# Starting every SBUF tile on a multiple of 128 bytes instead of 32 bytes past one

## The chip, the cores and the metric

The kernel runs on one core of one Trainium2 chip. The metric is the device time of one execution in microseconds (us), as the median of several runs. One core has five engines that matter here: TensorE (PE in the profile, its weight loads PEld), VectorE (DVE), ScalarE (ACT), GpSimd (POOL) and SyncE (SP), which issues every DMA of this kernel. SBUF is the on-chip memory that all of them work from. It has 128 partitions, and a tile occupies the same byte range in each of them, so one number, the tile's start address in bytes, says where it lies.

## The reference

```python
k_p = k.reshape(B, H, Sp, 8, D).mean(axis=3)      # q, k, v: (8, 8, 576, 64)
v_p = v.reshape(B, H, Sp, 8, D).mean(axis=3)
scores = scale * np.matmul(q, k_p.transpose(0, 1, 3, 2))
attn = softmax(scores)                             # over Sp = 72 pooled keys
x = np.matmul(attn, v_p)                           # -> (4608 tokens, 512)
...
h = x @ w_in                                       # 512 -> 2048
g = np.where(h >= 1, h, np.where(h <= -1, 0.0, (h + 1) ** 2 / 4))
x = g @ w_out                                      # 2048 -> 512
...
h = x @ w_in2
r = np.maximum(h, 0.0)
out = (r * r) @ w_out2
```

An attention over pooled keys and values is followed by two feed-forward layers, each 512 to 2048 to 512, over 4608 tokens, all in fp32.

## The kernel before

**Stages.** In the first 40 us the kernel loads k, v, q and the first weights and does the attention of the first 512 tokens. Then come 9 blocks of 512 tokens of the first layer, 16 steps each (`steps`). A step is one `gemm1` (line 675, 128 hidden columns) and, two steps later, one `gemm2` (line 747). Attention of the tokens ahead (lines 319 to 510) is put into slots between the steps, and the second layer's weights are prepared and written to DRAM. Block 0 of the second layer runs through the same two functions with weights streamed back into tiles `wt`. The other 8 blocks of the second layer are done in pairs by a seven-product (Strassen) scheme, whose matmuls stand at line 1017 (first product) and line 1026 (second product).

**Matmuls.** Accuracy is kept by splitting each operand into a rounded high part and a remainder, both of type fp32r, and multiplying three times: high by high, low by high, high by low. Every such matmul has a 128x128 stationary operand (512 bytes per partition) and 512 moving columns (2048 bytes per partition):

```python
for a, c in ((wh, xh), (wh, xl), (wl, xh)):
    ...
    nc.tensor.matmul(out=ph, lhsT=a[:, kk % a.shape[1], :], rhs=c[:, kk, :], ...)
```

The moving operand is one run of 2048 bytes, except in `gemm2` of the second layer's block 0. There the weights move, and they are two runs of 1024 bytes, 2048 bytes apart, of a `wt` tile. The first 10 steps of `gemm2` (line 736) use plain fp32 operands and one matmul instead of three.

**Where tiles lie.** Each matmul pairs tiles from pools that grow from the left (low) end of SBUF or from the right (high) end. Left: `cv` (staged weights `st`, `cb`, `z`), `xp` (`xhi`, `xlo`), `gp` (`gh`, `gl`), `ap`, `ac`, `kvp`, `at`, `wq` (`wt`) and, in the Strassen part, `gq`, `gs` (`gh`, `gl` again) and `tp`. Right: `wp`, `ws` (`wihi`, `wilo`, `wohi`, `wolo`) and, in the Strassen part, `wr` (`w`), `xc` (`x`) and `xt`. The left end begins with the pool `const`, which holds `ident` (512 bytes) and then `warm`, a constant of 4 bytes that takes a slot of 32:

```python
edge = ctx.enter_context(tc.tile_pool(name="edge", bufs=1, side="right"))
edge.tile([P, 16], F32, name="edge")
...
warm = const.tile([P, 1], F32, name="warm")
```

`const` begins at byte 16,512, which is 129 x 128, so the first pool after it begins at 16,512 + 512 + 32 = 17,056, which is 32 past a multiple of 128. At the right end the tile `edge`, which nothing reads or writes, keeps 64 bytes free, so that `wp` begins at byte 163,744, also 32 past a multiple of 128. Nearly every other tile has a size that is a multiple of 128 bytes and so inherits the 32. Only `ident` starts on a multiple of 128, and 54 tiles of 32 bytes in the pool `at` take all four residues in turn.

**Order.** Instruction order on each engine is fixed by the program. Address overlaps between pools that are closed and pools that take their place decide which instruction waits for which.

Of the kernel before, what the change touches and what calls it, by code (L numbers as in the profile page):

```python
# [10 lines left out]
F32 = mybir.dt.float32  # L11
# [22 lines left out]
def pooled_attention_moe_moe(  # L34
# [17 lines left out]
    P = 128  # L52
# [11 lines left out]
    const = ctx.enter_context(tc.tile_pool(name="const", bufs=1))  # L64
# [1 line left out]
    left, right, attn = ExitStack(), ExitStack(), ExitStack()  # L66

    edge = ctx.enter_context(tc.tile_pool(name="edge", bufs=1, side="right"))
    edge.tile([P, 16], F32, name="edge")
    wp = right.enter_context(tc.tile_pool(name="wp", bufs=1, side="right"))  # L70
    ws = right.enter_context(tc.tile_pool(name="ws", bufs=2, side="right"))
    cv = left.enter_context(tc.tile_pool(name="cv", bufs=4))
# [21 lines left out]

    ON_PE = 2
    NK = -(-SP // TR)
    warm = const.tile([P, 1], F32, name="warm")
    pad = [ac.tile([P, NK, H, TR], F32, name=f"pad{i}") for i in range(2)]

    def runs(t0, n):  # L100
# [1073 lines left out]
```

## Time and profile before

| | |
|---|---|
| median of 3 runs | 1637.45 us (1637.22 to 1638.47) |
| profiled execution | 1638.23 us, its span 1636.4 us |
| mean granted TensorE clock | 0.996 |
| busy share of the span | PE 99%, PEld 80%, DVE 77%, ACT 55%, POOL 7% |
| DMA | 284.67 MB, mean 174 GB/s |

The span runs from the first to the last instruction; 1.8 us of the execution's time lie around it. PE's busy time contains the modelled ends of pipelined matmuls, so its rate is read from starts: the time of a group of matmuls in the chain of work divided by their number.

### The profile page before, as it was taken

Reading aid. Unit: us, or ns where it says so; the run is one execution under the profiler, and the core shown is the slowest. Engines: PE = TensorE matmul, PEld = TensorE weight load, DVE = VectorE, ACT = ScalarE, POOL = GpSimd, SP = SyncE. Lnnn points to the kernel's source line nnn. Section 1 sums busy time; section 2 is a strip of 40 time slices with the busy share of each in tenths; the row PEclk is TensorE's granted clock in tenths of the full one; section 3 lists DMA queues with packets and bytes.
Section 4 is the critical chain, followed back from the end, with each engine's and each line's share of the span. In section 5 each row is a group of like instructions: output and inputs, shape, how many; then the busy total and the mean of one; then the engine's idle time right before and its main releaser. Section 6 shows DMA issues by size and latency. Waiting matters only on the chain.

```text
span 1636.4 us, 23224 instructions
## 1 busy us (share of the span) xinstructions
PE 1614.0 (99%) x7824; PEld 1314.2 (80%) x7824; DVE 1259.9 (77%) x2230; ACT 896.7 (55%) x1612; POOL 107.4 (7%) x91
## 2 busy tenths in 40 slices
PE   7999999999999999999999999999999999999998
PEld 6667888888878888888888888888888888888886
DVE  6999888898898988898885452579558855975585
ACT  6665556666666666666675532345435533553353
POOL 1442001011001000000100000000000000000000
PEclk9999999999999999999999999999999999999999
DMA  9565335545454554544370284667676776758564
GB/s 244 175 202 133 97 75 167 155 153 155 138 159 144 164 148 134 155 147 160 130 270 7 88 280 148 194 217 210 194 255 220 209 233 213 224 180 252 195 206 132
DMA packets 246725, 284.67 MB, mean 174 GB/s; under 512 B 121168, under 2 KB 149840, under 8 KB 246608
## 3 DMA queue, kind: packets, MB, share of 16 engines
q1 hardware_dynamic: 246608, 283.21, 56.5%
q8 instruction: 62, 1.02, 0.3%
q14 instruction: 55, 0.45, 0.1%
HBM read 218.10 MB, written 65.01 MB: 173 GB/s over the span
## 4 chain that ended last, share of the span: by engine, by line
PE 92%; DVE 4%; ACT 1%; DMA 1%; issue 1%; SPq 0%; POOL 0%; DVEq 0%; ACTq 0%; POOLq 0%
PE ph L675 25%; PE acc L747 25%; PE cp L1017 10%; PE dp L1026 10%; PE dq L1026 5%; PE cr L1017 5%; PE cq L1017 3%; PE dr L1026 3%; PE px L497 2%; PE pss L381 2%; PE acc L736 1%; DVE wi L155 0%; DMA kv<-in_k_dram 0%; DVE wilo L233 0%; DMA st<-in_moe_w_in_dram 0%
## 5 line engine op out<-in xcount | busy, mean ns | idle before, releaser
L675 PE MATMUL ph<-xhi,wihi 128*128 128x512 f32 x576 | 229.9, 399 | 0.9 <-ACT xhi L509 0.9
L974 ACT ACTIVATE gh<-g 128x512 fp32r<-128x512 f32 x224 | 140.7, 632 | 155.0 <-DVE g L1043 48.0
L675 PE MATMUL ph<-xlo,wihi 128*128 128x512 f32 x576 | 224.6, 390 | 0.0
L675 PE MATMUL ph<-xhi,wilo 128*128 128x512 f32 x576 | 224.5, 390 | 0.0
L747 PE MATMUL acc<-gh,wohi 128*128 128x512 f32 x536 | 215.8, 403 | 0.0
L747 PE MATMUL acc<-gl,wohi 128*128 128x512 f32 x536 | 209.5, 391 | 0.0
L747 PE MATMUL acc<-gh,wolo 128*128 128x512 f32 x536 | 209.0, 390 | 0.0
L782 DVE TENSOR_TENSOR gl<-g,gh 128x512 fp32r<-128x512 f32 x224 | 151.9, 688 | 49.6 <-ACT gh L974 48.1
L1017 PE MATMUL cp<-x,w 128*128 128x512 f32 x768 | 186.2, 390 | 0.2
L1017 PEld LDWEIGHTS cp<-x,w 128*128 128x128 f32 x768 | 143.9, 188 | 31.3 <-ACT s L1039 1.4
L1026 PE MATMUL dp<-gh,w 128*128 128x512 f32 x512 | 161.6, 389 | 0.0
L229 ACT ACTIVATE wihi<-wi 128x512 fp32r<-128x512 f32 x144 | 90.6, 629 | 122.0 <-PE ph L675 118.9
L233 DVE TENSOR_TENSOR wilo<-wi,wihi 128x512 fp32r<-128x512 f32 x144 | 104.4, 725 | 47.3 <-ACT wihi L229 46.9
L675 PEld LDWEIGHTS ph<-xhi,wihi 128*128 128x128 f32 x576 | 108.0, 188 | 27.8 <-issue 3.7
L675 PEld LDWEIGHTS ph<-xhi,wilo 128*128 128x128 f32 x576 | 108.1, 188 | 23.2 <-issue 0.2
L675 PEld LDWEIGHTS ph<-xlo,wihi 128*128 128x128 f32 x576 | 108.2, 188 | 21.8 <-issue 0.5
L1039 ACT ACTIVATE s<-cp 128x512 f32<-128x512 f32 x96 | 57.2, 596 | 116.4 <-PE cp L1017 116.4
L710 ACT ACTIVATE gh<-g 128x512 fp32r<-128x512 f32 x134 | 84.4, 630 | 66.3 <-DVE g L708 64.5
L747 PEld LDWEIGHTS acc<-gl,wohi 128*128 128x128 f32 x536 | 100.6, 188 | 22.4
L716 DVE TENSOR_TENSOR gl<-g,gh 128x512 fp32r<-128x512 f32 x150 | 103.4, 690 | 18.5 <-ACT gh L710 15.9
L747 PEld LDWEIGHTS acc<-gh,wohi 128*128 128x128 f32 x536 | 100.7, 188 | 20.4 <-issue 1.0
L747 PEld LDWEIGHTS acc<-gh,wolo 128*128 128x128 f32 x536 | 100.8, 188 | 19.4
(144 smaller groups left out, 3015.5 us busy)
## 6 DMA issues: line engine op xcount, KB each, us to landing
w<-w2i SPq DMA_DIRECT2D x224, 256.0 KB
w<-w2o SPq DMA_DIRECT2D x224, 256.0 KB
w2i<-cb SPq DMA_DIRECT2D x32, 512.0 KB
w2o<-cb SPq DMA_DIRECT2D x32, 512.0 KB
st<-in_moe_w_out_dram SPq DMA_DIRECT2D x31, 512.0 KB
st<-in_moe_w_in_dram SPq DMA_DIRECT2D x29, 512.0 KB
pd<-pad SPq DMA_DIRECT2D x32, 384.0 KB
z<-pd SPq DMA_DIRECT2D x96, 128.0 KB
```

The costliest lines, as they stand in the source:

```text
L229: nc.scalar.activation(out=hi, in_=src, func=AF.Copy)
L233: eng.tensor_tensor(out=lo, in0=src, in1=hi.bitcast(F32), op=ALU.subtract)
L381: nc.tensor.matmul(out=pss[off:off + n, i, :], lhsT=qT[t][:, p, off:off + n], rhs=kbd[b % 2][:, p, :], start=True, stop=True,)
L675: nc.tensor.matmul(out=ph, lhsT=a[:, kk % a.shape[1], :], rhs=c[:, kk, :], start=(i == 0), stop=(i == 3 * KD - 1))
L710: act(out=gh, in_=g, func=AF.Copy)
L716: nc.vector.tensor_tensor(out=gl, in0=g, in1=gh.bitcast(F32), op=ALU.subtract)
L747: nc.tensor.matmul(out=o, lhsT=lhsT, rhs=rhs, start=(f == 0 and x == 0), stop=(f == KF - 1 and x == 2),)
L782: tt(out=out, in0=a, in1=b, op=ALU.subtract)
L974: act(out=hi, in_=a, func=AF.Copy)
L1017: nc.tensor.matmul(out=out[0], lhsT=w[:, a, k, :], rhs=xq[b, i][c][:, k, :], start=(n == 0 and i in (1, 2, 7)), stop=(n == 5), skip_group_ ...
L1026: nc.tensor.matmul(out=out[d], lhsT=w[:, a, d, :], rhs=x[c], start=(g == 0 and n == 0 and i in (1, 2, 7, 4)), stop=(g == NG - 1 and n == 2 ...
L1039: act(out=snaps[key], in_=a, func=AF.Copy)
```

## The change

```diff
     edge = ctx.enter_context(tc.tile_pool(name="edge", bufs=1, side="right"))
-    edge.tile([P, 16], F32, name="edge")
+    edge.tile([P, 24], F32, name="edge")
...
-    warm = const.tile([P, 1], F32, name="warm")
+    warm = const.tile([P, 32], F32, name="warm")[:, 0:1]
```

`warm` takes 128 bytes where it took a slot of 32, so every tile on the left side moves up by 96 bytes: `cv` begins at 17,152 = 134 x 128. `edge` keeps 96 bytes free where it kept 64, so every tile on the right side moves down by 32 bytes: `wp` begins at 163,712 = 1279 x 128. In the built program all tiles except 54 of the 32-byte tiles in `at` then begin on a multiple of 128. The instructions of every engine, their order and the semaphores that they wait for are the same, row for row, in both programs, so no piece of the order is shown: only addresses differ. Between two tiles on the same side nothing changes; between a left tile and a right tile the distance shrinks by 128 bytes.

## Rows read from the trace of the kernel before

**Rows 1.** The profile's page: span, busy times, chain that ended last by engine.
```profile
span 1636.4 us, 23224 instructions
...
PE 1614.0 (99%) x7824; PEld 1314.2 (80%) x7824; DVE 1259.9 (77%) x2230; ACT 896.7 (55%) x1612; POOL 107.4 (7%) x91
...
PE 92%; DVE 4%; ACT 1%; DMA 1%; issue 1%; SPq 0%; POOL 0%; DVEq 0%; ACTq 0%; POOLq 0%
```

**Rows 2.** Busy time of each engine by stage (columns in the first line).
```profile
core 0: us, PE busy (x) PEld busy (x) DVE busy (x) ACT busy (x) POOL busy (x), PEclk, DMA share, GB/s
0.00:40.00 40.00, 31.15 (x245) 27.38 (x245) 23.79 (x56) 23.96 (x71) 6.57 (x14) 0.91 0.99 243
40.00:120.00 80.00, 75.19 (x462) 50.63 (x464) 78.81 (x127) 51.40 (x96) 38.95 (x24) 1.00 0.64 189
...
200.00:830.00 630.00, 630.00 (x3207) 514.30 (x3205) 561.84 (x1088) 411.51 (x750) 50.31 (x45) 1.00 0.48 148
...
1020.00:1636.40 616.40, 608.95 (x2683) 502.90 (x2681) 427.32 (x673) 275.34 (x458) 0.00 (x0) 1.00 0.67 209
```

**Rows 3.** Chain that ended last, in order of time: start us, us, work.
```profile
2.04 6.39 DMA kv<-in_k_dram
...
94.50 4.88 DMA st<-in_moe_w_in_dram
116.10 3.44 PE acc L736 x8
...
1010.59 8.16 PE acc L747 x36
1024.19 4.08 PE cp L1017 x18
...
1105.79 10.88 PE dq L1026 x48
...
1626.43 2.99 DMA out_dram<-o
```

**Rows 4.** Lines 675, 747, 1017, 1026: matmuls with count, duration ns min/median/max.
```profile
L675 PE MATMUL ph<-xhi,wihi x576: 389/389/796, 40.0 to 922.7; 128*128 128x512 f32 x192
...
L675 PE MATMUL ph<-xhi,wt x128: 389/389/389, 926.1 to 1010.2; 128*128 128x512 f32 x128
...
L747 PE MATMUL acc<-gh,wohi x536: 389/389/504, 137.1 to 936.3; 128*128 128x512 f32 x179
...
L747 PE MATMUL acc<-wt,gh x128: 389/389/389, 939.7 to 1018.1; 128*128 128x512 f32 x128
...
L1017 PE MATMUL cp<-x,w x768: 389/389/497, 1018.6 to 1552.6; 128*128 128x512 f32 x192
...
L1026 PE MATMUL dp<-gh,w x512: 388/389/389, 1092.0 to 1628.7; 128*128 128x512 f32 x171
```

**Rows 5.** PE in order of time, first layer, after two attention matmuls.
```profile
257.67 0.29 PE L324 MATMUL pk<-ident,kp 72*128 72x72 f32 x2
257.76 0.48 PE L675 MATMUL ph<-xhi,wihi 128*128 128x512 f32 x1
258.08 0.40 PE L675 MATMUL ph<-xlo,wihi 128*128 128x512 f32 x1
258.31 0.40 PE L675 MATMUL ph<-xhi,wilo 128*128 128x512 f32 x1
...
260.39 0.39 PE L675 MATMUL ph<-xhi,wilo 128*128 128x512 f32 x1
```

## The prediction

> **What bounds the kernel now.** I read the page first: TensorE is busy for 1614.0 of 1636.4 us, and 92% of the chain that ended last is its own work [rows 1]. Then the stages. From 200 us to the end TensorE is hardly without a matmul until the last one, while VectorE has 68 us of slack in the longest stage (561.84 of 630) and the DMA engines run at half to two thirds [rows 2]. Only the first 120 us are different: up to 40 us the DMA engines are full (0.99), and from 40 to 120 us VectorE is (78.81 of 80).
>
> So the rate of the matmuls is what a move of addresses has to change if it is to change the time. I read it from groups in the chain. In the second layer 48 matmuls take 10.88 us, 18 take 4.08 and 36 take 8.16 [rows 3]: 226.7 ns each, all three times. [...] How many pay it: at line 675 three groups of 576 (the first shown) and 128 + 64 with `wt`, 1920 in all; at line 747 three of 536 and 128 + 64, 1800; at line 1017 768 + 384 + 192 = 1344; at line 1026 512 + 256 for `dp`, 256 + 128 for `dq`, 128 + 64 for `dr`, 1344 [rows 4]. The sum is 6408, and 6408 x 226.7 ns = 1453 us, 89% of the span.
>
> **The change, part by part.** It adds no instruction, removes none and adds no wait. `warm` is set and read once, its one column as before, at no cost. What can change is what an access costs at its new address.
>
> *Moving operand.* All 6408 start 32 bytes past a multiple of 128. [...] I take 0 here. [...]
>
> [...]
>
> [...]
>
> *Left against right.* Where one operand is on the left and the other on the right, their distance was a multiple of 256 bytes and becomes 128 past one. This holds for 3 x 576 + 3 x 536 + 1344 = 4680 matmuls. The 1344 of line 1017 (both right) and the 384 with `wt` (both left) keep their distance. Nothing in the trace shows that distance matters: left-right pairs (`dq`), right-right (`cp`) and left-left (`acc` with `wt`) all have 226.7 ns [rows 3]. I take 0; what a bad pairing could cost is bounded below.
>
> *DMA.* A faster transfer counts only where the chain goes through it: 6.39 us for the first k, 4.88 us for a staged weight at 94.5 us and 2.99 us for the last store [rows 3], 14.3 us together. Elsewhere TensorE covers it. No transfer of the trace has an aligned tile, so the gain has bounds only: nothing, and, taking a quarter of it as the far end, since the bytes themselves stay, 3.6 us. I take 0.5 us, near the lower end, because a tile's packets are long against 32 bytes (2 KB per partition in the k loads). The other side, a slower transfer, I bound at the same 0.5 us.
>
> [...]
>
> *VectorE, ScalarE, GpSimd.* Their accesses move along with the tiles. After 200 us TensorE hides them. From 40 to 120 us VectorE is full, so 1% of its durations would be 0.8 us, either way. Every tile that they stream keeps its distance to the others of its side, so I take 0.
>
> Sum: 1638.23 - 0.5 = 1637.7 us for the profiled execution, which was 0.8 us above the median of the runs. On the median that is **1637.0 us**.
>
> **Rivals.** [...]
>
> *The left-right distance matters, and 128 is a bad one.* For it: the rate is not always locked at 226.7 ns. After two small attention matmuls the fp32r matmuls run from 258.08 to 260.39 in 10 steps of 231 ns with the same operands, and then settle [rows 5]. So two reads of TensorE, the load of the next weights and the moving operand, may get into each other's way, depending on how they fall. If the new distance kept them in the worse pattern, 4680 x (231 - 226.7) = 20 us would be added: 1657.5 us. From 0.7 ns per matmul on (3.3 us) the kernel is slower by more than the bound below. Against it: the three kinds of pairing now run alike.
>
> *A small gain at the start.* The transfers of the chain gain their quarter: 1634 us.
>
> *The change doesn't do what it says.* The addresses of the built program, given above, rule this out for all operands of the 6408 matmuls.
>
> **How the numbers follow.** No change: 0.56; it covers 1634.2 to 1640.7, which is 0.2% (3.3 us) either way, about what a measurement of this kernel can tell from no change. The large gain, by either way: 0.17. A small gain beyond 0.2%, by the transfers or by a part of the 13.3 ns: 0.08. A loss by the left-right distance, whole or in part: 0.19. The prediction is the likeliest, 1637.0 us. Leaving out the large gain (0.17) and the outer ends of the small gain and of the loss (0.03 together), the range is 1624 to 1658 us: its upper end is the full loss, its lower end a sixth of the large gain. From the same cases: faster 0.25, same 0.56, slower 0.19.
>
> **What would show it.** Right: groups of 48 matmuls of lines 1017 and 1026 in the chain still take 10.88 us (or 18 take 4.08), and the first start of line 675 stays near 40.0 us. [...] Wrong by the loss: `dq` and `acc` with `wohi` rise above 227 ns while `cp` does not. With faster matmuls the next bound would be VectorE from 200 to 830 us, which has 68 us of slack there, and the first 120 us would not shrink.

## The result: slower by 1.3%

The changed kernel takes 1658.82 us in the median of 4 runs (1658.28 to 1659.25); the kernel before, timed beside it, 1637.34 us. The ratio is 1.013, with a 95% interval of 1.0113 to 1.0148. The profiled execution's span is 1656.3 us against 1636.4.

The page of the changed kernel answers to [rows 1]:

```profile
span 1656.3 us, 23224 instructions
...
PE 1636.1 (99%) x7824; PEld 1314.0 (79%) x7824; DVE 1262.4 (76%) x2230; ACT 898.0 (54%) x1612; POOL 107.1 (6%) x91
```

The count of instructions is the same, and VectorE, ScalarE and GpSimd are busy for the same time within 2.5 us. TensorE alone has grown, by 22.1 us. The stages of the changed kernel, with the columns of [rows 2], show where it is felt:

```profile
200.00:830.00 630.00, 630.00 (x3148) 506.94 (x3147) 554.84 (x1071) 406.05 (x739) 49.97 (x44) 1.00 0.46 144
...
1020.00:1656.30 636.30, 629.91 (x2735) 512.72 (x2733) 431.24 (x679) 278.33 (x464) 0.00 (x0) 1.00 0.65 204
```

At the same granted clock of 1.00, 3148 matmuls fit into the 630 us where 3207 did. The chain of the changed kernel, in order of time, answers to [rows 3]:

```profile
1022.37 8.17 PE acc L747 x36
1035.98 4.08 PE cp L1017 x18
...
1117.91 11.20 PE dq L1026 x48
```

This is the reading that decides. `cp` (both operands on the right) still takes 4.08 / 18 = 226.7 ns and `acc` with `wt` (both on the left) 8.17 / 36 = 226.9 ns. `dq`, with its moving operand on the left and its stationary operand on the right, went from 10.88 to 11.20 us for 48, so from 226.7 to 233.3 ns. In the first layer a group of line 747 (`acc` with `wohi` and `wolo`, again left against right) that no attention matmul disturbs took, in the kernel before and in the changed one,

```profile
225.37 2.72 PE acc L747 x12
```

```profile
229.57 2.79 PE acc L747 x12
```

so it went from 226.7 to 232.5 ns each. The matmuls of line 675 in the changed kernel, in order of time:

```profile
301.33 0.40 PE L675 MATMUL ph<-xhi,wihi 128*128 128x512 f32 x1
301.57 0.39 PE L675 MATMUL ph<-xlo,wihi 128*128 128x512 f32 x1
301.80 0.40 PE L675 MATMUL ph<-xhi,wilo 128*128 128x512 f32 x1
...
303.90 0.39 PE L675 MATMUL ph<-xhi,wilo 128*128 128x512 f32 x1
```

From 301.33 to 303.90 there are 11 steps in 2.57 us, 234 ns each, with no attention matmul ahead of them. In the kernel before such steps were seen only for a while after an attention matmul [rows 5]: between 150 and 900 us its starts lie 226.7 ns apart from the twelfth matmul behind one on.

The counts and the starts by line answer to [rows 4]:

```profile
L675 PE MATMUL ph<-xhi,wihi x576: 387/393/796, 37.3 to 934.2; 128*128 128x512 f32 x192
...
L1017 PE MATMUL cp<-x,w x768: 387/389/498, 1030.4 to 1571.3; 128*128 128x512 f32 x192
...
L1026 PE MATMUL dp<-gh,w x512: 392/395/398, 1103.8 to 1649.7; 128*128 128x512 f32 x171
```

From these starts the loss can be split. From the first matmul of line 675 to the first of line 1017 it took 1018.6 - 40.0 = 978.6 us and takes 1030.4 - 37.3 = 993.1: 14.5 us more. From there to the last matmul it took 610.1 us and takes 619.3: 9.2 us more. The first matmul of line 675 comes 2.7 us earlier. Together the last matmul comes 21.0 us later. The span grew by 19.9 us only, since what follows that start took 7.7 us before and takes 6.6.

### The profile page after: what moved, and what is told of

Read it like the earlier page. It is cut to its first block, busy times and chain, and to the rows that moved or that the text cites. A ratio compares the mean times of both kernels' runs of the same rounds, so it can differ in the third digit from the quotient of the medians.

```text
span 1656.3 us, 23224 instructions
## 1 busy us (share of the span) xinstructions
PE 1636.1 (99%) x7824; PEld 1314.0 (79%) x7824; DVE 1262.4 (76%) x2230; ACT 898.0 (54%) x1612; POOL 107.1 (6%) x91
## 4 chain that ended last, share of the span: by engine, by line
PE 91%; DVE 4%; DMA 3%; ACT 1%; SPq 1%; issue 1%; POOL 0%; DVEq 0%; ACTq 0%; POOLq 0%
PE ph L675 25%; PE acc L747 25%; PE dp L1026 11%; PE cp L1017 10%; PE dq L1026 5%; PE cr L1017 5%; PE dr L1026 3%; PE cq L1017 3%; PE pss L381 2%; PE px L497 2%; DMA st<-in_moe_w_in_dram 1%; DMA pd<-pad 1%; DMA kv<-in_v_dram 0%; SPq L265 0%; DMA kv<-in_k_dram 0%
## 5 line engine op out<-in xcount | busy, mean ns | idle before, releaser
L675 PE MATMUL ph<-xhi,wihi 128*128 128x512 f32 x576 | 233.3, 405 | 1.4 <-ACT xhi L509 1.4
L675 PE MATMUL ph<-xlo,wihi 128*128 128x512 f32 x576 | 228.1, 396 | 0.0
```

## The experiments

Theory A: the rate of an fp32r matmul depends on the distance between the start addresses of its two operands, modulo 256 bytes. All tiles of one side have the same start modulo 256, so the distance (stationary minus moving) was 0 in every one of the 6408 matmuls before, and became 128 in the 4680 left-right ones. Theory B, the rival: what costs is the start on a multiple of 128 itself. The edits below are against the kernel before; a tile takes the same place on its side unless the edit moves it.

**Aligned, with the distance put back.**

```diff
-    edge.tile([P, 16], F32, name="edge")
+    edge.tile([P, 56], F32, name="edge")
...
-    warm = const.tile([P, 1], F32, name="warm")
+    warm = const.tile([P, 32], F32, name="warm")[:, 0:1]
```

> All tiles begin on multiples of 128 as in the changed kernel, but 224 bytes are kept free at the right edge, so that the left-right distance is a multiple of 256 again. Theory A (the distance between the moving and the stationary operand, modulo 256, sets the matmul rate): 1637 us, within 0.3%, lines 747 and 1026 back at 226.7 ns. Theory B (the start on a multiple of 128 itself is what costs): 1659 us, with 231 to 233 ns there.

Measured: 1635.55 us (1634.43 to 1637.36, 10 runs), the kernel before beside it 1638.24; ratio 0.9985, interval 0.9976 to 0.9995. Its chain:

```profile
1104.31 10.88 PE dq L1026 x48
```

Everything starts on a multiple of 128, as in the changed kernel, and the loss is gone. Theory B falls.

**Not aligned, with the distance of the changed kernel.**

```diff
-    edge.tile([P, 16], F32, name="edge")
+    edge.tile([P, 48], F32, name="edge")
```

> All tiles begin 32 bytes past a multiple of 128 as in the kernel before, but 192 bytes are kept free at the right edge, so that the left-right distance is 128 modulo 256 as in the changed kernel. Theory A (distance): 1659 us, line 1026 at about 233 ns and line 1017 at 226.7. Theory B (start on 128): 1637 us and 226.7 ns everywhere.

Measured: 1660.98 us, ratio 1.0141 (1.0126 to 1.0156). Its chain has the changed kernel's times to within the last digit:

```profile
1035.98 4.08 PE cp L1017 x18
...
1117.90 11.20 PE dq L1026 x48
```

With no tile of the matmuls on a multiple of 128, the whole loss is there. A and B are told apart from both sides.

**One side moved alone.** First only the left (`warm` with 32 columns, `edge` as before), then only the right (`edge` with 24 columns, `warm` as before): the two halves of the change.

> Only the left side moves, by 96 bytes: the constant takes 128 bytes, the right edge keeps 64. The left-right distance is 160 modulo 256. Theory A: the 4680 left-right matmuls may take any rate between 226.7 and 233 ns, 1637 to 1668 us, and lines 1017 and 747 with wt stay at 226.7 ns. Theory B, if it is the moving operand on 128 that costs: the matmuls with wt go up too, to about 231 ns, and the time is 1659 us or more.

> Only the right side moves, by 32 bytes: the right edge keeps 96 bytes, the constant takes 4. The left-right distance is 224 modulo 256. Theory A: 1637 to 1668 us by the rate of the 4680 left-right matmuls alone; line 1017, where both operands move together, stays at 226.7 ns. Theory B, if it is the stationary operand on 128 that costs: line 1017 goes up to about 231 ns as well.

Measured: the left alone 1662.33 us, ratio 1.0151 (1.0135 to 1.0166); the right alone 1663.85 us, ratio 1.0161 (1.0146 to 1.0177). Each half costs as much as both together or a little more, so the parts don't add: what counts is where the two sides end up against each other. In the chain of the one with the right moved alone `cp` still takes 4.08 us for 18, so a stationary operand on 128 costs nothing of itself. In the chain of the one with the left moved alone the 36 matmuls of `acc` with `wt` still take 8.17 us, so a moving operand on 128 costs nothing of itself either. With the right moved alone:

```profile
1041.01 4.08 PE cp L1017 x18
...
1122.99 11.20 PE dq L1026 x48
```

**The other distances.** Four kernels that change only the columns of `edge`: 64, 72, 56 and 32 in place of 16. One run each.

> Kernel before with 256 bytes kept free at the right edge: left-right distance 64 modulo 256 (what it would be with nothing kept free). Theory A with a period of 256 and only 0 good: line 1026 at about 233.3 ns, about 1660 us. Theory A with a period of 64: 226.7 ns and 1637 us. [...]

> Kernel before with 288 bytes kept free at the right edge: left-right distance 32 modulo 256. Only 0 good: line 1026 at about 233.3 ns, about 1660 us. A better distance than 0 exists: below 226.7 ns.

> Kernel before with 224 bytes kept free at the right edge: left-right distance 96 modulo 256. Only 0 good: line 1026 at about 233.3 ns, about 1660 us. A better distance than 0 exists: below 226.7 ns.

> Kernel before with 128 bytes kept free at the right edge: left-right distance 192 modulo 256. Only 0 good: line 1026 at about 233.3 ns, about 1660 us. A better distance than 0 exists: below 226.7 ns.

Measured, with the times of 48 matmuls of line 1026 in each chain:

| distance mod 256 | 48 of line 1026, us | one, ns | time, us |
|---|---|---|---|
| 0 (before) | 10.88 | 226.7 | 1637.70 beside these four |
| 32 | 11.20 | 233.3 | 1664.99 |
| 64 | 11.20 | 233.3 | 1663.97 |
| 96 | 11.24 | 234.2 | 1673.00 |
| 128 (the change) | 11.20 | 233.3 | 1658.82 |
| 160 (left alone) | 11.20 | 233.3 | 1662.33 |
| 192 | 10.99 | 229.0 | 1645.47 |
| 224 (right alone) | 11.20 | 233.3 | 1663.85 |

Of the eight distances that steps of 32 bytes allow, 0 is the best, 192 comes next, and none is below 226.7 ns. The period is not 64 or 128. It is not longer than 256 either: by the addresses of the built kernel before, the distances of line 1026 are all odd multiples of 256 and those of line 1017 all even ones, and both lines run at 226.7 ns. The single time at 96 holds one thing more: its clock was lower for longer early on, 0.91 on the mean between 60 and 100 us (columns as in [rows 2]) where the kernel before had 1.00, so its rate is comparable and its time less so.

```profile
60.00:100.00 40.00, 38.37 (x196) 27.39 (x196) 35.95 (x59) 22.39 (x44) 15.27 (x11) 0.91 0.70 208
```

**A pair on one side.** Both operands of line 1017 lie on the right. 128 bytes between their pools move `x` against `w` and leave all left-right pairs alone.

```diff
-xc = ctx.enter_context(tc.tile_pool(name="xc", bufs=1, side="right", reuse_waits="tile"))
+ctx.enter_context(tc.tile_pool(name="gap", bufs=1, side="right")).tile([P, 32], F32, name="gap"); xc = ctx.enter_context(tc.tile_pool(name="xc", bufs=1, side="right", reuse_waits="tile"))
```

> Kernel before with 128 bytes left free between the pools wr and xc, both on the right: line 1017's moving operand x then lies 128 modulo 256 from its stationary operand w, while all left-right pairs keep 0. Theory A (distance of the two operands of a matmul, wherever they lie): line 1017 goes from 226.7 to about 233.3 ns, 1344 x 6.6 ns = 9 us, about 1646 us; line 1026 stays at 226.7. Rival (it matters which side a tile is on, or the start address of the right side as a whole): 1637 us, line 1017 unchanged.

Measured: 1645.11 us (6 runs), ratio 1.0042 (1.0028 to 1.0056), the kernel before beside it 1638.03. Its chain:

```profile
1023.13 4.20 PE cp L1017 x18
...
1106.84 10.88 PE dq L1026 x48
```

Now it is `cp` that pays, 4.20 / 18 = 233.3 ns, and `dq` does not. So it is a matter of the two operands of a matmul and not of sides. The time moved by 7.1 us where A expected 9; in the later passes of the same kernel 18 of `cp` take 4.18 or 4.19 us, a little less than at first. One thing the runs can't tell: the stationary operands that follow each other in one stretch all start alike modulo 256, so the one that counts may be a matmul's own or the next one, whose load falls into its time (in the kernel before, the load for the matmul of line 1026 that starts at 1118.09 us runs from 1117.87 to 1118.06).

**What sets the rate at the best distance.** At distance 0 a matmul of line 1026 takes 226.7 ns. Two kernels change line 1026, for the second matmul of each three: one loads half of the stationary columns, the other moves half of the moving columns. Each leaves that part of the product out.

```diff
-out=out[d], lhsT=w[:, a, d, :], rhs=x[c],
+out=out[d][0:P // (1 + (n == 1))], lhsT=w[:, a, d, 0:P // (1 + (n == 1))], rhs=x[c],
```

> Kernel before, where every second matmul of each three of line 1026 loads only 64 of its 128 stationary columns (that part of the product is left out). [...] Theory D (a fixed cost per matmul): 10.88 us as before.

```diff
-out=out[d], lhsT=w[:, a, d, :], rhs=x[c],
+out=out[d][:, 0:TB // (1 + (n == 1))], lhsT=w[:, a, d, :], rhs=x[c][:, 0:TB // (1 + (n == 1))],
```

> Kernel before, where every second matmul of each three of line 1026 moves only 256 of its 512 columns (that part of the product is left out). [...]

Measured, in the chain of the first and then of the second:

```profile
1108.54 11.03 PE dq L1026 x48
```

```profile
1103.16 9.39 PE dq L1026 x48
```

The single times are 1645.50 and 1599.98 us. With half the columns to load, the 48 matmuls became slower, 229.8 ns on the mean: a fixed cost (10.88) does not say that, and a cost that falls with the columns loaded says it less still. With half the columns moved, half the time for the halved matmuls would give 32 x 226.7 + 16 x 113.3 ns = 9.07 us, and 9.39 us is above it. PE in order of time in that kernel shows the parts:

```profile
1120.25 0.28 PE L1026 MATMUL dp<-gl,w 128*128 128x256 f32 x1
1120.37 0.63 PE L1026 MATMUL dp<-gh,w 128*128 128x512 f32 x2
1120.83 0.29 PE L1026 MATMUL dp<-gl,w 128*128 128x256 f32 x1
1120.96 0.63 PE L1026 MATMUL dp<-gh,w 128*128 128x512 f32 x2
```

Two full matmuls take 0.46 us, about 230 ns each, and the half ones 0.12 and 0.13 us. Over the 48, (9.39 - 32 x 0.230) / 16 = 0.127 us, above 113.3 ns by far: the time of a matmul did not halve with the columns moved. The full matmuls beside the halved ones run at about 230 ns and not at 226.7, so the edit changed more than the matmuls that it halved, and what a load costs by itself stays open.

**The aligned kernel at distance 0 once more.**

> The kernel of the first experiment once more, with more rounds: all tiles on multiples of 128 and the left-right distance 0 modulo 256. If starting on 128 is worth something by itself, it is again faster than the kernel before by about 0.15%, 1635.5 us. If the first result came from where the half-speed stretch of the clock fell in the first 60 us, the ratio is 1.000 within 0.1%.

Measured: 1636.75 us (11 runs) beside 1637.65, ratio 0.9989, interval 0.998 to 0.9998. Both results together put it about 0.1% below the kernel before. It is the fastest of the versions that do the whole work, but the gain is less than the 0.2% that the prediction took as the least that a measurement of this kernel can tell.

## Why the prediction was wrong

**The step that failed** is "Left against right": "Nothing in the trace shows that distance matters ... I take 0." The three kinds of pairing that it compared were no control at all. The text itself says that the left-right distance was a multiple of 256, and same-side pairs have distances that are multiples of 256 too. Three groups that share the value of the very thing in question can't say that it doesn't matter. The runs showed in its place that the distance modulo 256 sets the rate: 226.7 ns at 0 and about 233 at 128, with all tiles on 128 or none (the first two experiments), and with the two operands on different sides or on the same one (the pair on the right).

**The distance stood among the rivals**, and the signs given for it were right: `dq` and `acc` with `wohi` up, `cp` and `acc` with `wt` unchanged. Its price was 4.3 ns for each of 4680 matmuls, 20 us. Line 1026 lost 6.6 ns, 10.88 to 11.20 us for 48; with 1344 matmuls that is 9 us of the 9.2 measured behind the first start of line 1017. Lines 675 and 747 lost 14.5 us over 3336, 4.3 ns each on the mean: undisturbed groups of 12 lost about 6 ns each, but others ran slower than 226.7 ns before already, behind attention matmuls [rows 5], and nearly all of it was lost after 200 us. So the loss was 23.7 us, of which the start gave 2.7 back. The range ended at the full loss of that rival, 1657.5 us, and the measured 1658.8 lies just behind it. That the two are so close is in part luck: the price was too low for line 1026, and the earlier start, which is not the distance's, made up for much of that. Why the distance costs, which the prediction put down to two reads that may get into each other's way, no run shows.

**The alignment as a gain** was rightly given little weight: aligned tiles at distance 0 run at 226.7 ns as before. No run shows the 13.3 ns of its chances or the large gain that sets the lower end of its range; the runs showed in their place 226.7 ns (10.88 us for 48) as the shortest time of a whole matmul of line 1026, aligned or not, at any of the eight distances. What part of the 226.7 ns a load or the start of a matmul takes stays open.

**The start and the DMA.** The 2.7 us at the start follow neither the alignment nor the distance. In the changed kernel the clock is at 0.97 on the mean over the first 60 us, in the kernel before at 0.94 [rows 2 has 0.91 up to 40 us]; the stretch near half the granted clock was shorter: in steps of 2 us it has 0.67, 0.50, 0.50 and 0.63 from 30 to 38 us in the kernel before, and 0.63 and 0.51 from 38 to 42 us in the changed one. The kernel with nothing aligned and distance 128 also starts line 675 at 37.4 us, with 0.97. The aligned kernel at distance 0 was profiled in both ways: the first time it starts line 675 at 38.6 us with 0.97, and once more at 39.8 us with 0.94:

```profile
0.00:60.00 60.00, 49.09 (x399) 39.86 (x399) 43.32 (x85) 39.22 (x99) 15.07 (x20) 0.94 0.71 200
```

The 0.5 us for DMA can't be seen beside that. What makes the aligned kernel 0.1% faster at distance 0 was not isolated.

**VectorE** at no cost was right: `gl` at line 782 takes 688 ns in both kernels.

## What to carry to other kernels

Before two operands are called independent of their addresses, look for two groups in the trace that really differ in the address relation in question; if all share it, the trace is silent, and a small change to an allocation should be priced by the worst pattern seen anywhere in the trace at the least (here that was 4.3 ns, and line 1026 lost 6.6). Where TensorE is the bound and both operands of its fp32r matmuls stream from SBUF, choose pool starts so that stationary and moving tiles start at the same address modulo 256. Here 32 bytes more at the right end were enough to lose 1.6%; the 1.5% that 96 bytes more at the left end cost came back, and a little more, with 224 bytes in place of 64 kept free at the right. Both were shown for 128x128 by 512 matmuls with a load for each, and for no other shape.

## What the runs showed of the hardware

The rate of a 128x128 by 512 fp32r matmul, with one load of the stationary operand for each, depends on the distance of its operands modulo 256 bytes: on line 1026 226.7 ns at 0, 229.0 at 192, 233.3 to 234.2 at the other multiples of 32, at a granted clock of 1.00. At 128 the starts fall into a lasting rhythm of long and short steps: from 1118 us on, line 1026 of the changed kernel takes 229 and 237 or 238 ns by turns, where the kernel before takes 226 or 227.

Plain fp32 shows nothing of the kind. The operands of line 736 lie left against right too, and in the chain 8 of its matmul records take 3.44 us in the kernel before [rows 3]; at a distance of 128 (nothing aligned) and at 96 they take

```profile
113.77 3.44 PE acc L736 x8
```

```profile
90.44 3.43 PE acc L736 x8
```

that is about 430 ns each at every one of these distances. The trace has two such records for each plain fp32 matmul of the program (80 for 40).

So the 430 ns of plain fp32 did not move with the distance, while moving the two operands of an fp32r matmul against each other by 128 bytes costs 6.6 ns of 226.7 on line 1026. Why the distance counts was not shown; the two runs with half an operand did not settle it.
